# Linear attention and a top-1 mixture of experts on one core: remainders of up to 64 tokens join the chunk ahead as a fourth half tile, remainders of 65 to 192 take a tile from it, and the narrow body goes

## The chip, the cores and the metric

The kernel runs on one core of one Trainium2 chip. The metric is the device time of one execution in microseconds; the time before is 680.21 us, the median of three runs (679.69 to 680.33). Engines are named as the profile names them: PE (matmul) and PEld (its weight loads), DVE (vector), ACT (scalar), POOL (GpSimd) and SP (which issues most DMAs).

## The reference

Eight batches of eight heads with 576 positions of 64 dimensions go through a linear attention with 128 random features; the result, 4608 tokens of 512 numbers, goes through a mixture of eight experts of which each token uses the one with the largest gate logit.

```python
def phi(x):
    proj = np.einsum('bhsd,md->bhsm', x, omega)
    h = proj - np.sum(x * x, axis=-1, keepdims=True) / 2.0
    return np.exp(h - np.max(h, axis=-1, keepdims=True)) / np.sqrt(m)
q_p, k_p = phi(q * scale), phi(k * scale)
kv, z = np.einsum('bhsm,bhsd->bhmd', k_p, v), np.sum(k_p, axis=2)
num = np.einsum('bhsm,bhmd->bhsd', q_p, kv)
den = np.einsum('bhsm,bhm->bhs', q_p, z)[..., None] + 1e-06
x = (num / den), as rows of tokens (4608 x 512)
logits = x @ w_gate;  expert_idx = argmax(logits);  gate_w = softmax(logits)[expert_idx]
for e in range(8):
    ye = np.maximum(x[expert_idx == e] @ w1[e], 0.0) @ w2[e]      # 512 -> 1024 -> 512
    out[expert_idx == e] = gate_w[...] * ye
```

## The kernel before

The first part (some 245 us) is attention, one unit for each batch and head, with the gate's logits worked out beside it. Tokens are written to DRAM as rows (`token_rows`) with the softmax weight at the end. The routing ranks each token within its expert.

The second part is the experts. Tokens of an expert are cut into chunks of T3 = 384 (A3 = 3 tiles of P = 128). Chunk t's tokens are fetched by indirect DMA through a table of slots, `idx`, that `slots` makes: one-hot matrices of the tokens' slots (`T1`, line 740) are multiplied on PE with matrices that hold the tokens' numbers (`RH`, line 748). A front of T2 = 256 tokens of the expert that leads after half the batches is worked out early, in single precision, while the routing goes on. `plan` then works out flags for each chunk: its expert's number and whether it changes, whether the chunk exists, how many tokens it has. All engines load these flags into registers and branch on them.

Matmuls of the chunks run in fp32r with operands split into a high and a low part. Layer 1 (`layer1`, `wide`, `l1`) takes 96 matmuls a chunk: eight blocks of 128 features, 12 matmuls each, with n columns, where n is 384, 320 or 256 by the tokens; two blocks (a group g) share a pair of PSUM banks, `p_1[g % 2]`, which `hid` empties with ACT and DVE. A chunk of up to 192 tokens goes through the narrow body (`slim`, lines 1025 to 1029): 64 matmuls, high and low part of the tokens side by side. Layer 2 (`layer2`, line 1060) takes 24 matmuls of 512 columns a tile (`triple`), or 16 for a half tile of up to 64 tokens (`l2` with `half`); tiles of a chunk that hold no token are skipped by a branch (line 1064).

`step(t)` is layer 1 and layer 2 of a chunk on PE, then on the others the weights of chunk t+1, the gather of chunk t+3 (POOL), `begin(t+1)` and the output of chunk t (`out2`: ACT scales a whole tile; for a half tile ACT, DVE and DVE; POOL scatters the rows to the output, line 1079). `begin(t)` moves chunk t+1 through DRAM (`move`, SP), starts loads of the next expert's weights, splits new weights where the expert changes (`change`, `split`), and turns chunk t+1's rows (`xrows`, `xtrans`: a transpose on DVE, a cast on ACT, a subtraction on DVE for each tile). Where the chunk before was narrow, `xrows` waits for layer 1 of the next instead (lines 1056 to 1058).

The order on each engine is that of the program text. `Routing.constants` runs after the first unit of attention: POOL makes the iotas and masks, DVE takes token numbers from one of them (lines 474 to 478), and `clear` sets the gather buffer to zero.

Of the kernel before, what the change touches and what calls it, by code (L numbers as in the profile page):

```python
# [8 lines left out]
F32 = mybir.dt.float32  # L9
# [28 lines left out]
NCL = -(-(NT - T2) // T3)  # L38
NCH = (NT - T2 + E * (T3 - 1)) // T3
NQ = NCH + 2  # L40
NS = A3 * NCH
# [375 lines left out]
class Routing:  # L417
# [10 lines left out]
    def setup(self):  # L428
# [7 lines left out]
        self.RH = self.oh.tile([P, NLT, 2, P], BF16, name="rt_RH")  # L436
        self.EX = t("rt_EX", [P, GT, E + 1])
# [13 lines left out]
    def constants(self):  # L451
# [4 lines left out]
        nc.vector.tensor_copy(self.iob, self.iop)  # L456
        nc.gpsimd.iota(self.rev, pattern=[[-1, E]], base=E, channel_multiplier=0, allow_small_or_imprecise_dtypes=True)
# [76 lines left out]
    def group(self, bs, g, sl, lr):  # L534
# [114 lines left out]
    def head(self, nb, idx, flags):  # L649
# [5 lines left out]
        v = t("v", [P, 4 * E])  # L655
        mx, mw, io, lo = v[:, :1], v[:, 1:2], v[:, 2:4], v[:, 4:6]
        w, sel, ns = (v[:, i * E:(i + 1) * E] for i in range(1, 4))
        self.sel = sel
# [41 lines left out]
        def f6():  # L700
            nc.vector.tensor_scalar(out=ns, in0=sel, scalar1=-1.0, scalar2=1.0, op0=ALU.mult, op1=ALU.add)
            nc.vector.tensor_tensor(out=self.low, in0=self.low, in1=sel.unsqueeze(1).to_broadcast([P, E, E]), op=ALU.max)
            nc.vector.tensor_tensor(out=self.low, in0=self.low, in1=ns.unsqueeze(2).to_broadcast([P, E, E]), op=ALU.mult)
# [15 lines left out]
    def slots(self, banks, idx, fill):  # L719
# [6 lines left out]
        cnt, c2, off, m, nn = t("cnt", [P, E]), t("c2", [P, E]), t("off", [P, E]), t("m", [P, E, E]), t("nn", [P, E])  # L726
        nc.vector.scalar_tensor_tensor(out=nn, in0=self.sel, scalar=-float(T2), in1=pn[:, :E], op0=ALU.mult, op1=ALU.add)
        nc.vector.tensor_scalar(out=cnt, in0=nn, scalar1=1.0 / T3, scalar2=FLOOR3, op0=ALU.mult, op1=ALU.add)
        nc.vector.tensor_scalar(out=c2, in0=cnt, scalar1=BIG, scalar2=-BIG, op0=ALU.add, op1=ALU.add)
        cb = c2.unsqueeze(1).to_broadcast([P, E, E])  # L730
        nc.vector.tensor_tensor(out=m, in0=self.low, in1=cb, op=ALU.mult)
        nc.vector.tensor_reduce(out=off, in_=m, axis=AX.X, op=ALU.add)
        nc.vector.scalar_tensor_tensor(out=cnt, in0=off, scalar=1.5, in1=self.sel, op0=ALU.mult, op1=ALU.subtract)
        so, tt = t("so", [P, NLT, E]), t("tt", [P, NLT])
        nc.vector.tensor_tensor(out=so, in0=self.OH.rearrange("p g s e -> p (g s) e"),
                                in1=cnt.unsqueeze(1).to_broadcast([P, NLT, E]), op=ALU.mult)
        nc.vector.tensor_reduce(out=tt, in_=so, axis=AX.X, op=ALU.add)
        nc.vector.scalar_tensor_tensor(out=tt, in0=tt, scalar=2.0, in1=self.RT.rearrange("p g s -> p (g s)"),
                                       op0=ALU.mult, op1=ALU.add)
        T1 = t("T1", [P, NLT, NS], BF16)  # L740
        for c in range(0, NLT, GT):
            nc.vector.tensor_tensor(out=T1[:, c:c + GT, :], in0=tt[:, c:c + GT].unsqueeze(2).to_broadcast([P, GT, NS]),
                                    in1=self.iop[:, :NS].unsqueeze(1).to_broadcast([P, GT, NS]), op=ALU.is_equal)
        for f, eng in self.tail:
            f(eng)
        for n, pp in enumerate((pa, pb)):
            for c in range(NLT):
                nc.tensor.matmul(pp[:, :NS], self.RH[:, c, n, :], T1[:, c, :], start=c == 0, stop=c == NLT - 1)
# [3 lines left out]
        self.off, self.c2, self.nn = off, c2, nn  # L752

    def plan(self, flags):


        nc, t, inc = self.nc, self.t, self.t("inc", [1, E])
        nc.vector.tensor_tensor(out=inc, in0=self.off[:1], in1=self.c2[:1], op=ALU.add)
        ge, eq, et = t("ge", [1, NQ, E]), t("eq", [1, NQ, E]), t("et", [1, NQ])
        io = self.iop[:1, :NQ].unsqueeze(2).to_broadcast([1, NQ, E])  # L760
        nc.vector.tensor_tensor(out=ge, in0=io, in1=inc.unsqueeze(1).to_broadcast([1, NQ, E]), op=ALU.is_lt)
        nc.vector.tensor_tensor(out=eq, in0=io, in1=self.off[:1].unsqueeze(1).to_broadcast([1, NQ, E]), op=ALU.is_ge)
        nc.vector.tensor_tensor(out=eq, in0=eq, in1=ge, op=ALU.mult)
# [12 lines left out]
        nc.vector.tensor_scalar(out=nx, in0=nx, scalar1=1.0, scalar2=-1.0, op0=ALU.max, op1=ALU.mult)
        nc.vector.tensor_scalar_add(nx, nx, float(E))
        nt, en, sb = t("nt", [1, NQ]), t("en", [1, E]), t("sb", [1, NQ])
        pick = t("pick", [1, NQ, E])
        nc.vector.tensor_tensor(out=pick, in0=eq, in1=nx.unsqueeze(1).to_broadcast([1, NQ, E]), op=ALU.mult)  # L780
        nc.vector.tensor_reduce(out=nt, in_=pick, axis=AX.X, op=ALU.add)
        nc.vector.scalar_tensor_tensor(out=en, in0=self.off[:1], scalar=float(T3), in1=self.nn[:1], op0=ALU.mult, op1=ALU.add)
        nc.vector.tensor_tensor(out=pick, in0=eq, in1=en.unsqueeze(1).to_broadcast([1, NQ, E]), op=ALU.mult)
        nc.vector.tensor_reduce(out=sb, in_=pick, axis=AX.X, op=ALU.add)
        nc.vector.scalar_tensor_tensor(out=sb, in0=self.iop[:1, :NQ], scalar=-float(T3), in1=sb, op0=ALU.mult, op1=ALU.add)
        nc.vector.tensor_scalar(out=sb, in0=sb, scalar1=0.0, scalar2=float(T3), op0=ALU.max, op1=ALU.min)
        for i, a in ((0, ch), (1, nt), (2, act), (4, sb)):
            nc.vector.tensor_copy(flags[:, i, :], a)


class Experts:
# [7 lines left out]
    def __init__(self, tc, ctx, rt, xs, w1, w2, out, ident, ps):  # L799
# [8 lines left out]
        self.xg = [cp.tile([P, A3, ROW], F32, name="xg")]  # L808
# [5 lines left out]
        self.bounce = [self.nc.dram_tensor(f"chunk_rows{i}", (T3, DM), F32, kind="Internal").ap() for i in range(2)]  # L814
        gt = cp.tile([P, 2 + 2 * A3], F32, name="gt")
        self.gt = [gt[:, i:i + 1] for i in range(2 + 2 * A3)]
# [103 lines left out]

    def gather(self, t):
        for a in range(A3):
            i = A3 * t + a
            self.nc.gpsimd.indirect_dma_start(out=self.xg[t % 2][:, a, :], out_offset=None, in_=self.xs[:, :],  # L924
                                              in_offset=bass.IndirectOffsetOnAxis(ap=self.idx[:, i:i + 1], axis=0),
                                              bounds_check=NT - 1, oob_is_err=False)
# [5 lines left out]
    def gate(self, t, a):  # L932
        return self.gt[2 + t % 2 * A3 + a]

    def weigh(self, t):
        self.weights(self.xg[t % 2], [self.gate(t, a) for a in range(A3)])

    def move(self, t):

        rows = self.bounce[t % 2]
        self.nc.sync.dma_start(rows.rearrange("(a p) n -> p a n", p=P), self.xg[t % 2][:, :, :DM])
        for q in range(4):
            self.nc.sync.dma_start(self.xq[q * Q:(q + 1) * Q],
                                   rows[:, q * P:(q + 1) * P].rearrange("(a g i) n -> i a g n", a=A3, i=Q))

    def xtrans(self, t, a):

        if t < NCH:  # L950
            x = self.xg[t % 2][:, a, :DM].rearrange("p (c t) -> p c t", t=P)
# [313 lines left out]
```

## Time and profile before

| | us |
|---|---|
| median of 3 runs | 680.21 (679.69 to 680.33) |
| the profiled execution | 679.88 |
| its span, first to last instruction | 678.2 |
| PE busy | 658.5 (97%) |
| DVE, ACT, POOL busy | 376.7, 359.2, 271.4 |

The profile is one execution, in which times count from the span's first instruction. Matmuls overlap in their pipeline, so the duration of one (0.33 to 0.39 us in the expert part) is longer than the time from one's start to the next one's; the text works with starts. In a row of the timeline stand start, busy time, engine, line, operation, output and inputs with their shapes, the number of merged instructions, and in brackets the idle time before it and what ended it.

### The profile page before, as it was taken

How to read it: one execution, taken by the hardware profiler on the slowest of the kernel's cores; microseconds unless marked ns; L12 is line 12 of the kernel's file. 1: busy time of each engine (PE TensorE's matmuls, PEld its weight loads, DVE VectorE, ACT ScalarE, POOL GpSimd, SP SyncE). 2: the span in 40 equal slices, each digit the busy share in tenths (PEclk: the TensorE clock that was granted, in tenths of full speed). 3: DMA queues.
4: the chain of work that ended last, by engine and by line, in shares of the span. 5: the costliest groups of instructions: out<-in, count | busy, mean ns of one | idle time of the engine just before them, and what ended most of it. 6: DMA issues, size and time to landing. Idle time of an engine off the chain costs nothing. (4 is left out here: it accounts for less than half of the span.)

```text
span 678.2 us, 19569 instructions
## 1 busy us (share of the span) xinstructions
PE 658.5 (97%) x7011; PEld 597.8 (88%) x7011; DVE 376.7 (56%) x729; ACT 359.2 (53%) x1082; POOL 271.4 (40%) x492
## 2 busy tenths in 40 slices
PE   8999999999999999999999999999999999999994
PEld 5999999999998987989898989898989888898983
DVE  4788888888887788632513265232455257332321
ACT  4999999999998935322222244222343254222121
POOL 6545557886787775041230304122112223122122
PEclk8999999999999999999999999999999999999998
DMA  7772835728493223747633456441457274541210
GB/s 221 222 231 67 269 112 175 234 59 261 114 350 131 43 77 96 233 146 251 157 94 115 105 196 159 178 120 58 103 188 243 105 214 128 197 119 45 54 49 10
DMA packets 93105, 100.51 MB, mean 148 GB/s; under 512 B 28942, under 2 KB 73486, under 8 KB 92304
## 3 DMA queue, kind: packets, MB, share of 16 engines
q1 hardware_dynamic: 85216, 79.27, 38.7%
q0 software_dynamic: 7040, 19.04, 9.0%
q8 instruction: 89, 1.46, 0.9%
q14 instruction: 72, 0.59, 0.3%
q10 hardware_dynamic: 688, 0.16, 0.1%
HBM read 72.92 MB, written 29.77 MB: 151 GB/s over the span
## 5 line engine op out<-in xcount | busy, mean ns | idle before, releaser
L975 PE MATMUL p<-xb,w1p 128*128 128x384 f32 (+1 forms) x1056 | 183.4, 333 | 0.5 <-DVE xb L51 0.4
L975 PEld LDWEIGHTS p<-xb,w1p 128*128 128x128 f32 x1056 | 181.0, 188 | 2.3 <-issue 1.5
L1079 POOL DMA_INDIRECT out_dram<-ys,idx x38 | 38.2, 1005 | 269.4 <-DVEq L1069 79.9
L887 PE MATMUL p<-w2p,hb 128*128 128x512 f32 x552 | 127.1, 389 | 0.0
L1002 DVE SCALAR_TENSOR_TENSOR hb<-p,hb 128x768 fp32r<-128x768 f32 (+1 forms) x44 | 41.0, 932 | 154.5 <-ACTq L1110 96.3
L887 PEld LDWEIGHTS p<-w2p,hb 128*128 128x128 f32 x552 | 103.6, 188 | 21.5
L1001 ACT ACTIVATE hb<-p 128x768 fp32r<-128x768 f32 (+1 forms) x44 | 34.9, 793 | 110.0 <-PE p L975 109.7
L191 DVE TENSOR_REDUCE mx<-pp 128x8 f32<-128x1024 f32 x64 | 78.0, 1218 | 10.5 <-PE pp L185 9.8
L199 ACT ACTIVATE qp<-pp,mx 128x128 f32<-128x128 f32 x256 | 77.2, 435 | 0.0
L199 ACT ACTIVATE kp<-pp,mx 128x128 f32<-128x128 f32 x256 | 74.1, 385 | 5.0 <-DVE de L283 1.4
L185 PE MATMUL pp<-omt,th 64*128 64x128 f32 x1024 | 72.1, 281 | 0.0
L185 PEld LDWEIGHTS pp<-omt,th 64*128 64x128 f32 x1024 | 63.4, 191 | 0.0
L887 PE MATMUL p_1tr<-w2p,hb 128*128 128x512 f32 x240 | 57.0, 391 | 0.6 <-DVEq L1110 0.5
L211 POOL TENSOR_TENSOR k<-kp 128x256 f32<-128x256 f32 x64 | 46.7, 729 | 23.7 <-ACT kp L199 18.7
L887 PEld LDWEIGHTS p_1tr<-w2p,hb 128*128 128x128 f32 x240 | 44.8, 188 | 10.3 <-DVEq L1110 0.9
L176 DVE COPY th<-tr 128x512 f32<-128x512 f32 x63 | 43.3, 687 | 5.1 <-PE tr L168 3.3
L274 PE MATMUL nu<-kva,qt 128*64 128x73 f32 x1008 | 46.0, 233 | 0.0
L243 ACT COPY qt<-t 128x512 f32<-128x512 f32 x64 | 42.3, 661 | 2.0 <-PE t L168 1.5
L274 PEld LDWEIGHTS nu<-kva,qt 128*64 128x64 f32 x1008 | 36.7, 136 | 4.2
L225 PE MATMUL kf<-kp,v 128*64 128x128 f32 x512 | 39.4, 275 | 0.0
L924 POOL DMA_INDIRECT xg<-token_rows,idx x24 | 26.4, 1100 | 30.2 <-DVEq L1110 17.3
L57 ACT CAST xb<-xgm 128x512 fp32r<-128x512 f32 x21 | 13.0, 621 | 45.6 <-DVE xgm L952 44.7
(387 smaller groups left out, 1063.4 us busy)
## 6 DMA issues: line engine op xcount, KB each, us to landing
w1s<-in_moe_w_dram SPq DMA_DIRECT2D x5, 2048.0 KB, 8.6
w2s<-in_moe_w_dram SPq DMA_DIRECT2D x5, 2048.0 KB, 11.0
xq<-chunk_rows SPq DMA_DIRECT2D x52, 192.0 KB, 4.3
v<-in_v_dram SPq DMA_DIRECT2D x32, 256.0 KB, 5.7
token_rows<-x SPq DMA_DIRECT2D x8, 1024.0 KB, 8.4
k<-in_k_dram SPq DMA_DIRECT2D x31, 256.0 KB, 5.2
q<-in_q_dram SPq DMA_DIRECT2D x31, 256.0 KB, 5.5
chunk_rows<-xgm SPq DMA_DIRECT2D x7, 768.0 KB, 4.6
```

The costliest lines, as they stand in the source:

```text
L176: self.nc.vector.tensor_copy(t.rearrange("p n (a t) -> p a n t", a=2), s[("tr", h)])
L185: nc.tensor.matmul(o[:, a, n, :], t[r, n, :], self.om[r], start=True, stop=True)
L191: self.nc.vector.tensor_reduce(out=mx, in_=s[("pp", h)], axis=AX.X, op=ALU.max, negate=True)
L199: self.nc.scalar.activation(o[:, j, :], p[:, a, 2 * n + i, :], AF.Exp, bias=mx[:, a, 2 * n + i:2 * n + i + 1])
L211: nc.gpsimd.tensor_tensor(out=k2, in0=kp[:, :2, :], in1=kp[:, 2:, :], op=ALU.add)
L225: nc.tensor.matmul(pkv[c * D:(c + 1) * D, :M], vv, kk, start=n < 2, stop=n > 2)
L243: self.nc.scalar.copy(qt.rearrange("p n (a t) -> p a n t", a=2), s[("t2", h)])
L274: nc.tensor.matmul(o[r, j, :], qt[:, j, r], kva[:, h if h >= 0 else 2 * j + a, :], start=True, stop=True)
L887: self.nc.tensor.matmul(p, x, w[:, c, :], start=c == 0 and x is h and w is self.w2h, stop=c == self.NF - 1 and x is l)
L975: self.nc.tensor.matmul(o, w[:, c, k], x[:, c, :], start=i == 0, stop=i == len(ops) - 1)
L1002: self.nc.vector.scalar_tensor_tensor(out=l, in0=p, scalar=0.0, in1=h.bitcast(F32), op0=ALU.max, op1=ALU.subtract)
L1079: self.nc.gpsimd.indirect_dma_start(out=self.out[:, :], in_=y, in_offset=None, bounds_check=NT - 1, out_offset=bass.IndirectOffsetOnAxis(a ...
```

## The change

- The chunks: an expert's remainder of up to 64 tokens behind its last full chunk joins that chunk as a half tile (T4 = 448 columns, `idx` gets a slot for each chunk's half tile, `p_2` a fourth bank, `gather`, `weigh`, `move`, `xrows` and `out2` a fourth part). A remainder of 65 to 192 is made larger: the chunk ahead gives one tile of 128 to it.
- `slim`, `l1_both` and `hid_both` go; layer 1 has bodies of 384, 448, 320 and 256 columns.
- The routing (`slots`): more small operations find the chunks' counts; the one-hot matrix is transposed, in bf16, and compared with a table `sn` that POOL makes in `constants`.
- `plan` is cut into three pieces; two of them run between the groups of chunk 0's layer 1. The load of the next expert's w1 is issued after that layer.
- `xrows(t + 1)` stands in `begin` without a condition.
- `hb` and `hq` move to a pool of their own, `h0` shares the memory of `xq`.

```diff
+T4 = T3 + HT
-NCL = -(-(NT - T2) // T3)
+NCL = -(-(NT - T2 - (E - 1) * HT) // T3)
-NS = A3 * NCH
+NM = A3 * NCH
+NS = NM + NCH
...
     def constants(self):
         nc.vector.tensor_copy(self.iob, self.iop)
+        nc.gpsimd.tensor_copy(self.sn[:, :NM], self.iop[:, :NM].unsqueeze(2).to_broadcast([P, NM, NLT]))
+        nc.gpsimd.tensor_scalar(out=self.sn[:, NM:], in0=self.iop[:, 1:NCH + 1].unsqueeze(2).to_broadcast([P, NCH, NLT]),
+                                scalar1=float(A3), scalar2=64.0, op0=ALU.mult, op1=ALU.add)
...
-            self.tail = [(f, nc.vector if i % 2 == 0 or i == 17 else nc.scalar if i < 8 else nc.gpsimd)
+            self.tail = [(f, nc.scalar if i % 2 and i < 12 else nc.vector if i < 16 and i % 2 == 0 else nc.gpsimd)
...
     def slots(self, banks, idx, fill):
+        for i, k in enumerate((1.0, 64.0)):
+            nc.scalar.activation(so[:, i, :, E:E + 1], rank.unsqueeze(2), AF.Copy, scale=k)
+        V.scalar_tensor_tensor(out=cnt, in0=self.sel, scalar=float(HT - T2), in1=pn[:, :E], op0=ALU.mult, op1=ALU.add)
...
+        V.scalar_tensor_tensor(out=X[:, 1], in0=b, scalar=8192.0, in1=c1, op0=ALU.mult, op1=ALU.add)
+        for i in range(2):
+            V.tensor_tensor(out=so[:, i, :, :E], in0=oh, in1=X[:, i].unsqueeze(1).to_broadcast([P, NLT, E]), op=ALU.mult)
+        for i in range(2):
+            V.tensor_reduce(out=v2[:, i], in_=so[:, i, :, :E + 1], axis=AX.X, op=ALU.add)
...
-        T1 = t("T1", [P, NLT, NS], BF16)
-        for c in range(0, NLT, GT):
-            nc.vector.tensor_tensor(out=T1[:, c:c + GT, :], in0=tt[:, c:c + GT].unsqueeze(2).to_broadcast([P, GT, NS]),
-                                    in1=self.iop[:, :NS].unsqueeze(1).to_broadcast([P, GT, NS]), op=ALU.is_equal)
+        for c in range(0, NLT, 2 * GT):
+            V.tensor_tensor(out=T1[:, :, c:c + 2 * GT], in0=tt[:, c:c + 2 * GT].unsqueeze(1).to_broadcast([P, NS, 2 * GT]),
+                            in1=self.sn[:, :, c:c + 2 * GT], op=ALU.is_equal)
...
     def gather(self, t):
-        for a in range(A3):
+        for a in range(A3 + (t > 0)):
...
     def xrows(self, t):
-        for a in range(A3):
+        for a in range(A3 + 1):
             self.xtrans(t, a)
...
     def layer1(self, t):
-            self.either(r > T2, lambda: self.either(r > T3 - HT, wide(T3), wide(T3 - HT)),
-                        lambda: self.either(r > T2 - HT, wide(T2), lambda: self.slim(t, g)))
+            self.either(r > T3 - HT, lambda: self.either(r < T3 + 1, wide(T3), wide(T4)),
+                        lambda: self.either(r > T2, wide(T3 - HT), wide(T2)))
             if g == 1 and t == 1:
                 self.xrows(t + 1)
-            elif g == 1:
-                with self.tc.If(self.before < T2 - HT + 1):
-                    self.xrows(t + 1)
...
     def layer2(self, t):
+        if t:
+            with self.tc.If(self.r4 > T3):
+                self.l2(A3, True)
         for a in range(A3 - 1, 0, -1):
             with self.tc.If(self.r4 > a * P):
                 one(a)
...
     def begin(self, t):
         if 1 < t < NCH - 1:
-            with self.tc.If(self.r2 > T2 - HT):
-                self.xrows(t + 1)
+            self.xrows(t + 1)
...
     def step(self, t, following):
         if t == 0:
-            self.first(T3)
+            self.first(T3, self.pieces)
+            self.next(0, 1)
...
-        for a in range(A3 - 1, -1, -1):
+        for a in range(A3 - (t == 0), -1, -1):
             self.out2(t, a, r, r2)
```

## Rows read from the trace of the kernel before

**Rows 1.** The page: engines' busy time; wide layer 1's group.
```profile
PE 658.5 (97%) x7011; PEld 597.8 (88%) x7011; DVE 376.7 (56%) x729; ACT 359.2 (53%) x1082; POOL 271.4 (40%) x492
...
L975 PE MATMUL p<-xb,w1p 128*128 128x384 f32 (+1 forms) x1056 | 183.4, 333 | 0.5 <-DVE xb L51 0.4
```
**Rows 2.** Timeline of PE, chunk 6 into chunk 7.
```profile
468.86 16.83 PE L975 MATMUL p<-xb,w1p 128*128 128x384 f32 x96
485.52 5.64 PE L887 MATMUL p_1tr<-w2p,hb 128*128 128x512 f32 x24
...
501.88 16.83 PE L975 MATMUL p<-xb,w1p 128*128 128x384 f32 x96
```
**Rows 3.** The same, chunk 3 (303 tokens) into chunk 4, where the expert changes.
```profile
373.80 14.24 PE L975 MATMUL p<-xb,w1p 128*128 128x320 f32 x96
387.88 3.81 PE L1036 MATMUL p_1tr<-w2p,hq 128*128 128x512 f32 x16
...
402.41 17.22 PE L975 MATMUL p<-xb,w1p 128*128 128x384 f32 x96
```
**Rows 4.** The same, the last chunk: end of layer 1, and layer 2.
```profile
664.37 0.36 PE L982 MATMUL p<-xb,w1p 128*128 128x384 f32 x1
665.61 3.94 PE L1036 MATMUL p<-w2p,hq 128*128 128x512 f32 x16 [0.87 <-PEq L1064]
```
**Rows 5.** Timeline of DVE behind the last matmul.
```profile
670.35 0.68 DVE L1092 TENSOR_TENSOR yt<-p,yt 64x512 f32<-64x512 f32 x1 [3.30 <-ACT yt L1091]
671.12 0.48 DVE L1093 TENSOR_SCALAR ys<-yt,gt 64x512 f32<-64x512 f32 x1
```
**Rows 6.** Timeline of PE, chunk 8 (narrow): layer 1 into layer 2.
```profile
544.33 0.36 PE L982 MATMUL p<-xb,w1p 128*128 128x384 f32 x1
545.33 3.94 PE L1036 MATMUL p<-w2p,hq 128*128 128x512 f32 x16 [0.64 <-PEq L1064]
```
**Rows 7.** Line 1064 on PE's queue, in 544:546 and 663:667 (ns min/median/max, first, last).
```profile
L1064 PEldq EVENT_SEMAPHORE  x1: 51/51/51, 544.7 to 544.7; - x1
L1064 PEldq COMPARE_BRANCH  x1: 70/70/70, 544.9 to 544.9; - x1
...
L1064 PEldq COMPARE_BRANCH  x2: 208/1090/1973, 662.3 to 664.9; - x2
L1064 PEldq EVENT_SEMAPHORE  x2: 51/51/51, 664.8 to 665.2; - x2
```
**Rows 8.** Timeline of POOL at the start: iotas, memset of the gather buffer.
```profile
5.68 0.25 POOL L455 IOTA rt_iop<- 128x128 f32 x1
...
7.95 0.33 POOL L471 IOTA rt_id<- 64x4 int32 x2
8.33 1.40 POOL L809 MEMSET xg<- 128x1560 f32 x1
```
**Rows 9.** Timeline of DVE there: the first operation on rt_id.
```profile
9.34 0.49 DVE L474 TENSOR_SCALAR rt_part<-rt_id 128x36 int32<-128x36 int32 x1
```
**Rows 10.** Timeline of PE there.
```profile
11.22 0.34 PE L168 MATMUL tr<-ident,k 64*128 64x64 f32 x4 [1.96 <-DVE th L176]
```
**Rows 11.** Groups of POOL's instructions by form: busy, mean ns | idle before.
```profile
L631 POOL TENSOR_SCALAR rt_RH<-rt_iob,rt_RM,rt_ihi 128x128 bf16<-128x128 bf16 x23 | 18.4, 798 | 0.1
```
**Rows 12.** Timeline of DVE in the routing, from the count to the one-hot.
```profile
248.30 0.23 DVE L588 TENSOR_TENSOR m<-rr,rt_OH 128x72 f32<-128x72 f32 x1 [0.73 <-PE rr L515]
...
250.25 0.46 DVE L735 TENSOR_TENSOR f_so<-rt_OH,f_cnt 128x288 f32<-128x288 bf16 x1
...
251.46 2.60 DVE L742 TENSOR_TENSOR f_T<-f_tt,rt_iop 128x513 bf16<-128x513 f32 x4
```
**Rows 13.** Timeline of PE there: the slots' matmuls.
```profile
255.22 2.25 PE L748 MATMUL p<-f_T,rt_RH 128*128 128x57 bf16 x72
```
**Rows 14.** Timeline of DVE: two tiles of xrows before chunk 7.
```profile
492.67 1.08 DVE L952 STREAM_TRANSPOSE xg<-xq 128x512 f32<-128x512 f32 x1
...
495.05 1.07 DVE L952 STREAM_TRANSPOSE xg<-xq 128x512 f32<-128x512 f32 x1
```

More of the change, by code (lines that the diff above doesn't have):

```diff
@@ new lines, in changes, with following @@
+        def changes():
+            T(out=ge, in0=eq, in1=self.iop[:1, :E].unsqueeze(1).to_broadcast(wide), op=ALU.mult)
+            V.memset(ch[:, :1], 0.0)
+            add(et, ge)
+            T(out=ch[:, 1:], in0=et[:, 1:], in1=et[:, :NQ - 1], op=ALU.not_equal)
+            T(out=flags[:, 0, 1:], in0=ch[:, 1:], in1=act[:, 1:], op=ALU.mult)
+            V.tensor_copy(flags[:, 0, :1], ch[:, :1])
+        def following():
+            V.tensor_single_scalar(nx, c2, 0.5, op=ALU.is_gt)
+            T(out=e8, in0=nx, in1=self.rev[:1], op=ALU.mult)
+            T(out=mm, in0=self.upp[:1], in1=e8.unsqueeze(1).to_broadcast([1, E, E]), op=ALU.mult)
+            V.reduce_max(out=nx, in_=mm, axis=AX.X)
+            V.tensor_scalar(out=nx, in0=nx, scalar1=1.0, scalar2=-1.0, op0=ALU.max, op1=ALU.mult)
+            V.tensor_scalar_add(nx, nx, float(E))
+            T(out=pick, in0=eq, in1=be(nx), op=ALU.mult)
+            add(nt, pick)
+            V.tensor_copy(flags[:, 1, :], nt)
@@ L791 @@
+        return [found, changes, following]
 class Experts:
@@ L1002, in high_low, with first @@
         self.nc.vector.scalar_tensor_tensor(out=l, in0=p, scalar=0.0, in1=h.bitcast(F32), op0=ALU.max, op1=ALU.subtract)
-    def hid_both(self, g, n, k):
-        nc, f = self.nc, slice(2 * g, 2 * g + 2)
-        p, y = self.p_1[g % 2][:, :, :2 * n].rearrange("p f (s t) -> p f s t", t=n), self.hs[g % 2]
-        nc.scalar.copy(y, p[:, :, 1])
-        nc.vector.tensor_tensor(out=y, in0=p[:, :, 0], in1=y, op=ALU.add)
-        if k:
-            self.whole(f, k, y[:, :, :k])
-        self.half(f, y[:, :, k:k + HT])
-    def first(self, n):
+    def first(self, n, pieces):
         for g in range(self.NF // 2):
@@ L1018, in first @@
             self.wide(0, g, n)
+            if pieces:
+                pieces.pop(0)()
     def wide(self, t, g, n):
@@ L1096, in both @@
             if t == 0:
-                self.store(p, g, self.idx[:, i:i + 1])
+                self.store(p, g, i)
                 return
             y = self.y()
-            self.either(r2 > a * P + HT, lambda: nc.scalar.activation(y, p, AF.Copy, scale=g), lambda: half(y))
-            self.scatter(y, self.idx[:, i:i + 1])
+            if a < A3:
+                self.either(r2 > a * P + HT, lambda: nc.scalar.activation(y, p, AF.Copy, scale=g), lambda: half(y))
+            else:
+                half(y)
+            self.scatter(y[:self.span(a)], i)
         if a:
@@ L1211, in run @@
         self.move(1)
-        rt.plan(self.flags)
-        self.next(0, 1)
+        found, *self.pieces = rt.plan(self.flags)
+        found()
         for t in range(NCL - 1):
```

180 lines of the change are left out of this document (90 added, 90 removed).

## The prediction

> **What bounds the kernel now.** I read the page first, then the timeline of PE, then what stands before PE's few gaps. PE is busy 97% of the span, and 1056 matmuls of a wide layer 1 at 96 a chunk make 11 wide chunks [rows 1]. The rest of layer 1 is two narrow chunks. This agrees with the tokens, which I counted with the reference on its drawn inputs: 1711, 1152, 576 and 1169 for four experts. 256 of the first run ahead as chunk 0's front, so 1455 = 3x384+303, 1152 = 3x384, 576 = 384+192, 1169 = 3x384+17: 13 chunks, numbered 0 to 12 here.
>
> In the timeline of PE chunk 6 starts at 468.86 and chunk 7 at 501.88 with no gap: 16.66 us for layer 1, 16.36 for layer 2 [rows 2]. So a wide chunk is PE alone, 0.1735 us a matmul of 384 columns and 0.2272 for one of 512. The chunk of 303 runs with 320 columns: 14.08/96 = 0.1467 a matmul, 28.61 us in all [rows 3]. The two sizes give 0.00042 us a column; 256 columns should cost 0.120, 448 should cost 0.200. What PE does is what the end moves by, except where PE stands: at the first copies of attention, at the routing, at an expert's change, behind a skipped branch.
>
> **The chunks, what is gained.** The new rule gives 4, 3, 2 and 3 chunks: 576 becomes 256+320, and the last expert 384, 384, 448 (17 tokens in the half tile). Nothing changes before chunk 7. There, from 501.88 to the last matmul's end, 665.61+3.94 = 669.55 [rows 2, 4], stand 167.67 us. After:
> - 256: 96x0.120 + 48x0.2272 = 22.41.
> - 320: 28.61, as chunk 3.
> - 384 after a change of expert behind a 320: its layer 1 lasts 17.22 where 16.83 is usual [rows 2, 3], so 33.41. Then 384: 33.02.
> - 448: 96x0.2004 + 88x0.2272 = 19.24+19.99, and 0.16 for the last matmul's own end: 39.39.
>
> The sum is 156.8, a gain of 10.8. Layer 2 has as many matmuls as before, 344. Behind the last matmul the half tile needed ACT, DVE, DVE; now tile 0 is whole and ACT alone scales it. The two DVE operations, 0.68 and 0.48 with a handover of 0.09, go [rows 5]: 1.2. Gain 12.0.
>
> **Skips on PE, the largest cost.** layer2 now begins with a branch on r4 > T3 that only the 448 chunk takes; chunks 1 to 10 skip it. The trace has such skips on PE only in the narrow chunks. In the first the last layer-1 matmul starts at 544.33 and the next matmul at 545.33, idle 0.64 before it, put down to PE's queue at line 1064 [rows 6]. The rows of that line show why: a semaphore event at 544.7, just as the last matmul ends (544.33+0.36), then a branch at 544.9; with two skips there are two such events and 0.87 idle [rows 4, 7]. I read it so: a skipped body must post its semaphore, and the post waits until PE has run dry. All of PE's matmuls are queued behind it, and everything waits for PE. Start to start is 1.00 against a usual 0.17: 0.83 for one skip, 1.24-0.17 = 1.07 for two. About 0.14 of it is the taken jump into the half body (208 ns against 70 in the branch rows), which a 384 chunk doesn't make. So 0.69 for nine chunks, 0.14 more for the 320 of the new chunk 8, and 0.93 for the 256, which skips two: 6.2+0.15+0.9 = 7.3. Bounds: 5.2 if only the recorded idle counts (10x0.50+0.2), 8.5 at 0.83 each. A loss of nothing is a rival, below.
>
> **The constants, at the start.** Two operations enter POOL's queue between the iotas of rt_iop (5.68) and rt_id (until 8.28): a copy of 57x36 = 2052 elements and a multiply-add of 684. DVE's constants read rt_id, and behind them in DVE's order stands a copy of attention (line 176) for which PE already waits 1.96 us at 11.22 [rows 8 to 10]. Nothing hides this: the longer POOL takes, the later that copy. Price of the copy: the memset of 1560 at 1.40 gives 0.84 ns an element with its start, 1.9 us. The multiply-add: by the memset 0.8; by POOL's tensor_scalar of 128 elements at 0.80 us [rows 11], about 4.7 ns an element behind its start, 3.4. I take the middle, 2.0; X = 3.9. The first DVE constant on rt_id took 0.49 for 36 elements and ended at 9.83, as POOL's memset did (8.33+1.40) [rows 8, 9]. So DVE either waits for the iota alone (X-1.35 = 2.5) or for the grown memset too (X+0.46 = 4.4). I take 3.5; bounds 1.0 and 5.7.
> [...]
>
> **The routing.** From the count to the first one-hot operation DVE now has 13 small operations for 6, two products and two sums for one each, three closing ones for one. Before, the products began 1.95 us after the first operation at 248.30, with 16 small operations interleaved (some 0.13 each), and the one-hot at 251.46 [rows 12]. Seven more at 0.14 are 1.0, the second product and sum about 0.75, two more at the end 0.25: the one-hot starts 2.0 later. It has 2736 elements for 2052. The row gives 0.65 us for 513, so two of 1368 would be 3.1 at its rate; DVE's scaling of 512 elements in 0.48 [rows 5] is the cheapest rate of a row, giving 2.1. Between them I take 2.6, as long as before. PE reached line 748 at 255.22 without a wait [rows 13]; its later matmuls need the tail's rows, which DVE makes behind the one-hot, one fewer for PE's first half than before, so of the 2.0 I take 1.7 for PE. Bounds 0.5 and 2.6. Gather and turning follow idx and shift as a whole.
> [...]
>
> **A change of expert.** xrows turns a fourth, half tile. A tile takes 2.38 (492.67 to 495.05) [rows 14], the half some 1.3. Beside a wide layer 2 this is hidden; before chunk 4, and before the new chunk 9, DVE and ACT are late already (the 0.39 above). There 1.3 and a little ACT branch work come on top, while PE comes 0.8 later through its skip: 0.75 each, 1.5 together; bounds 0 and 2.8.
>
> **Edits costed at nothing.** The fourth gather and weight copy, and one more issue on SP: POOL is busy 40% [rows 1] and the gathers run two chunks ahead; if that cover went, each gather costs POOL about 1 us. The plan's pieces move behind layer 1's groups of chunk 0, where DVE has time. w1's load for the next expert is issued later on SP, behind move(1); its first reader is the split before chunk 4, at 402.41. h0 shares xq, so move(1)'s second step waits for layer 2 of the front, whose matmuls end before chunk 0 begins. Dropping the conditional xrows inside layer1 frees xq and xg earlier. The larger memset of xg[1] and the fourth gather delay only chunk 1's rows, a chunk ahead.
>
> **Sum.** -12.0+7.3+3.5+1.7+1.5 = +2.0 us. The profiled execution took 679.88 (span 678.2 and 1.7 around it), 0.33 below the median 680.21; on the median the change comes to 682.2.
>
> **Rivals.**
> 1. The new skip is free behind 384 columns, because PE's sequencer runs far enough ahead. For it: chunk 3 jumps into the half body with no gap [rows 3]. Against it: the event falls on the end of the last matmul both times. Then 682.2-7.3 = 675. It decides at 0.5 us a skip: below that the kernel is faster. Chance 0.17.
> 2. [...] Chance 0.20.
> 3. The stalls are dear: POOL's multiply-add at tensor_scalar's price and DVE held until the memset's end, 5.7 in place of 3.5; the routing at 2.6 for 1.7, the changes of expert at 2.8 for 1.5: 686.6. For it: the one tensor_scalar of size on POOL has that price. Chance 0.13.
> 4. The counts differ on the chip and 13 chunks stay: the gain is gone, some 692. Against it: the shapes of the trace fit the counts. Chance 0.03.
>
> **How the numbers follow.** The forecast has 0.47. About 0.2% (1.36 us) is what a measurement of this kernel can tell from no change: under 678.85 or over 681.57. Around 682.2 I give the forecast 0.29 slower, 0.15 within, 0.03 faster; rival 1 gives 0.15 faster and 0.02 within; rival 2 0.09 and 0.11; rivals 3 and 4 are slower. Faster 0.27, within 0.28, slower 0.45. The range 676 to 687 leaves out about half of rival 1, rival 4 and the edge of rival 3.
>
> **What would show it.** Chunks 1 to 10 of the new trace with a gap of about 0.5 between layer 1 and layer 2, put down to PE's queue, and ten events on that line: right; seamless chunks: rival 1. PE's gap near 11.22 grown from 2 to 5.5 us with DVE waiting for POOL: the start. A gap at line 748 of 1 to 2 us: the routing. 12 chunks, the last with 448 columns, and 157 us plus skips from the 256 chunk to PE's end: the gain. The prediction is wrong if skips cost under 0.5, or if a wait appears that no row of before has, such as DVE's xrows holding the 256 chunk.

## The result, and the profile after

The changed kernel takes 689.85 us (median of 4 runs, 689.28 to 690.62) against 679.95 beside it: a ratio of 1.0146, 95% interval 1.0129 to 1.0164. It is 9.9 us slower. The forecast was 682.2 with a range of 676 to 687: the sign is right, the size is not, and the time lies outside the range. The profiled execution took 690.15 us, with a span of 688.3 where the kernel before had 678.2; the 10.1 us between the spans can be taken apart at five points that both traces have.

| stretch | before | after | difference | forecast |
|---|---|---|---|---|
| start, to the count's matmul | 248.19 | 251.52 | +3.33 | +3.5 |
| routing, from there to layer 1 of chunk 0 | 20.10 | 30.25 | **+10.15** | **+1.7** |
| chunk 0 | 38.85 | 38.85 | 0 | 0 |
| chunks 1 to 6 | 194.74 | 198.37 | +3.63 | +4.9 |
| chunk 7 to the last matmul's end | 167.67 | 161.40 | -6.27 | -6.9 |
| behind it | 8.65 | 7.91 | -0.74 | -1.2 |

Five of the six terms came out within 1.3 us, though the first of them moves by more than a microsecond between profiles of the same start (see "The start" below). One, the routing, is 8.5 us off, which is about the whole error. The timeline of PE of the kernel after shows where (start us, duration us, engine, line, operation; lines are those of the new kernel: L771 is the old L748, L900 the old L859), with three rows of the kernel before behind it:

```profile
251.52 0.18 PE L733 MATMUL p<-rt_CU,rt_ones 128*128 128x8 bf16 x1
251.56 7.15 PE L900 MATMUL p<-x,w1s 128*128 128x256 f32 x32
258.55 10.56 PE L771 MATMUL p<-rt_T,rt_RH 128*128 128x76 bf16 x72
268.93 5.10 PE L900 MATMUL p<-x,w1s 128*128 128x256 f32 x12
273.87 4.46 PE L918 MATMUL p<-w2s,xq 128*128 128x512 f32 x10
...
248.19 0.18 PE L724 MATMUL p<-rt_CU,rt_ones 128*128 128x8 bf16 x1
257.31 2.84 PE L859 MATMUL p<-x,w1s 128*128 128x256 f32 x12
259.98 4.45 PE L877 MATMUL p<-w2s,h 128*128 128x512 f32 x10
```

From the count to the first slot matmul PE takes 7.03 us, exactly as before, and starts line 771 with no wait. But the 72 slot matmuls take 10.56 us where [rows 13] had 2.25, and the 12 layer-1 products behind them take 5.10 where the kernel before had 2.84. From start to start that is 10.38 for 2.09 and 4.94 for 2.67, +8.29 and +2.27; what stands between them and chunk 0 took 0.41 less (7.90 for 8.31), which makes the 10.15. VectorE did its part faster than the cheapest rate I had from a row (2.1), 1.65 us for the one-hot that took 2.60 in [rows 12], and its last row of the tail was there at 259.81:

```profile
256.36 1.65 DVE L765 TENSOR_TENSOR rt_T<-f_tt,rt_sn 128x1368 bf16<-128x1368 bf16 x2
```

Stretches of 2 us there (PE busy, weight loads, DVE, ACT and POOL with counts, then the granted clock, DMA share, GB/s):

```profile
260.00:262.00 2.00, 2.00 (x16) 1.65 (x15) 0.00 (x0) 0.00 (x0) 0.00 (x0) 1.00 0.00 0
...
264.00:266.00 2.00, 2.00 (x16) 1.79 (x15) 0.00 (x0) 0.00 (x0) 0.00 (x0) 0.50 0.03 8
...
274.00:276.00 2.00, 2.00 (x6) 0.82 (x5) 0.92 (x4) 1.94 (x6) 2.00 (x2) 1.00 0.63 173
```

And stretches of 3 us of line 771 alone (PE busy, weight loads, granted clock, DMA share, GB/s):

```profile
259.00:262.00 3.00, 3.00 (x23) 2.47 (x22) 1.00 0.00 0
...
264.00:267.00 3.00, 3.00 (x23) 2.69 (x22) 0.50 0.02 5
```

From 260 to 268 all other engines are idle, hardly anything is moved (DMA share 0.00 to 0.03), PE counts as busy throughout, and a stretch of 3 us touches 23 slot matmuls at a granted clock of 1.00 and 23 at 0.50. The rate of these matmuls did not change when the granted clock was halved. The halved clock does cost something afterwards: the 12 layer-1 products, at a granted clock of 0.50 to 272 and a mean of 0.60 from there to 274, take 0.41 us each from start to start, where the kernel before took 0.22 at 1.00. I read this as a "busy" PE waiting for its operand, which the profile doesn't call idle; the experiments test it.

The other stretches came out near the forecast. The start, on POOL and then on DVE:

```profile
5.99 1.90 POOL L461 CAST rt_sn<-rt_iop 128x2052 bf16<-128x2052 f32 x1
7.86 0.78 POOL L462 TENSOR_SCALAR rt_sn<-rt_iop 128x684 bf16<-128x684 f32 x1
11.03 1.83 POOL L850 MEMSET xg<- 128x2080 f32 x1
...
11.00 1.89 DVE L481 TENSOR_SCALAR rt_part<-rt_id 128x36 int32<-128x36 int32 x1 [1.50 <-POOL rt_id L478]
```

And the chunks: the skip in a chunk of 384 between layer 1 and layer 2, the 256, and the last one with 448 columns, after which a single ACT operation stands where [rows 5] had two of DVE:

```profile
372.00 5.71 PE L928 MATMUL p_1tr<-w2p,hb 128*128 128x512 f32 x24 [0.44 <-PEq L1081]
...
518.99 11.67 PE L1022 MATMUL p<-xb,w1p 128*128 128x256 f32 x96
531.75 11.18 PE L928 MATMUL p<-w2p,hb 128*128 128x512 f32 x48 [1.08 <-ACTq L1133]
...
640.59 19.61 PE L1022 MATMUL p<-xb,w1p 128*128 128x448 f32 x96
660.05 4.00 PE L1057 MATMUL p_1t<-w2p,hq 128*128 128x512 f32 x16
...
680.55 0.69 ACT L1121 ACTIVATE ys<-p,gt 128x512 f32<-128x512 f32 x1 [4.75 <-PE p L928]
```

### The profile page after: what moved, and what is told of

It is laid out like the page before. It is cut to its first block, busy times and chain, and to the rows that moved or that the text cites. A ratio compares the mean times of both kernels' runs of the same rounds, so it can differ in the third digit from the quotient of the medians.

```text
span 688.3 us, 19314 instructions
## 1 busy us (share of the span) xinstructions
PE 662.6 (96%) x6979; PEld 597.7 (87%) x6979; DVE 382.0 (55%) x755; ACT 359.3 (52%) x1089; POOL 283.3 (41%) x514
## 5 line engine op out<-in xcount | busy, mean ns | idle before, releaser
L1022 PE MATMUL p<-xb,w1p 128*128 128x384 f32 (+3 forms) x1152 | 195.1, 329 | 0.0
L1022 PEld LDWEIGHTS p<-xb,w1p 128*128 128x128 f32 x1152 | 191.5, 188 | 3.1 <-issue 0.8
L928 PE MATMUL p<-w2p,hb 128*128 128x512 f32 x576 | 132.6, 389 | 1.1 <-ACTq L1133 1.1
L1038 DVE SCALAR_TENSOR_TENSOR hb<-p,hb 128x768 fp32r<-128x768 f32 (+1 forms) x48 | 42.8, 891 | 157.4 <-ACTq L1133 80.9
L928 PEld LDWEIGHTS p<-w2p,hb 128*128 128x128 f32 x576 | 108.0, 188 | 23.7 <-ACTq L1133 1.3
L1037 ACT ACTIVATE hb<-p 128x768 fp32r<-128x768 f32 (+1 forms) x48 | 36.4, 759 | 109.3 <-PE p L1022 81.3
L928 PE MATMUL p_1tr<-w2p,hb 128*128 128x512 f32 x216 | 51.5, 393 | 3.2 <-PEq L1081 3.1
L928 PEld LDWEIGHTS p_1tr<-w2p,hb 128*128 128x128 f32 x216 | 39.9, 188 | 13.8 <-issue 4.5
L971 POOL DMA_INDIRECT xg<-token_rows,idx x31 | 32.4, 1045 | 22.4 <-DVE idx L774 14.1
L59 ACT CAST xb<-xgm 128x512 fp32r<-128x512 f32 (+1 forms) x24 | 13.6, 567 | 48.2 <-DVE xgm L999 43.8
```

What stands on the lines that cost most here:

```text
L928: self.nc.tensor.matmul(p, x, w[:, c, :], start=c == 0 and x is h and w is self.w2h, stop=c == self.NF - 1 and x is l)
L1022: self.nc.tensor.matmul(o, w[:, c, k], x[:, c, :], start=i == 0, stop=i == len(ops) - 1)
L1038: self.nc.vector.scalar_tensor_tensor(out=l, in0=p, scalar=0.0, in1=h.bitcast(F32), op0=ALU.max, op1=ALU.subtract)
```

## The experiments

**Theory.** The new one-hot T1 is stored [slots, token columns]. VectorE writes it in runs of 18 adjoining elements, but a slot matmul takes one token column of it, `T1[:, :, c]`, so that its 76 columns lie 36 elements of bf16, 72 bytes, apart. Before, `T1[:, c, :]` gave 57 columns side by side. **Rivals:** the 19 more columns, the later rows of the tail, or the longer chain of small operations.

### The layout turned back for TensorE alone

```
-        self.T1 = self.oh.tile([P, NS, NLT], BF16, name="rt_T1")
+        self.T1 = self.oh.tile([P, NLT, NS], BF16, name="rt_T1")
...
-            V.tensor_tensor(out=T1[:, :, c:c + 2 * GT], in0=...
+            V.tensor_tensor(out=T1[:, c:c + 2 * GT, :].rearrange("p c s -> p s c"), in0=...
...
-                nc.tensor.matmul(pp[:, :NS], self.RH[:, c, n, :], T1[:, :, c], ...
+                nc.tensor.matmul(pp[:, :NS], self.RH[:, c, n, :], T1[:, c, :], ...
```

> The kernel after, with one change: the one-hot T1 is stored slot by slot within each token column, so that the 76 columns which one slot matmul reads lie side by side, as the kernel before had them; VectorE writes them through a turned view. Theory (the stride is the price): in the kernel after each slot matmul reads its 76 columns 72 bytes apart, and that made the 72 matmuls take 10.56 us instead of 2.25 and let the granted clock fall behind them. Side by side they take 76/57 of 2.25 us, 3.0 us, the clock stays at 1.00, the 12 layer-1 products behind them are back from 5.10 to 2.84 us, and the time falls by 9 to 10.5 us, to 679.5 to 681. VectorE's comparison may go back from 1.65 to 2.6 us for its scattered writes. Rival (the 19 more columns, or the later half-tile rows of the right operand, hold TensorE): the matmuls still span over 8 us and the time stays at 688 to 691.

Measured: 690.43 us, 1.0153 (1.0132 to 1.0175): no gain at all. By its total the rival would stand. The timelines of DVE and PE, and a stretch of 2 us at a granted clock of 0.50, say otherwise:

```profile
256.99 11.87 DVE L765 TENSOR_TENSOR rt_T<-f_tt,rt_sn 128x1368 bf16<-128x1368 bf16 x2
...
263.07 1.32 PE L771 MATMUL p<-rt_T,rt_RH 128*128 128x76 bf16 x18 [3.75 <-DVE rt_T L765]
268.91 3.87 PE L771 MATMUL p<-rt_T,rt_RH 128*128 128x76 bf16 x54 [4.52 <-DVE rt_RH L638]
...
270.00:272.00 2.00, 2.00 (x29) 1.76 (x29) 0.29 (x2) 0.00 (x0) 0.00 (x0) 0.50 0.00 0
```

TensorE now needs 3.71 us for 54 matmuls (to 272.62, where the next begin), 0.069 each on average, nearly all of it at a granted clock of 0.50, where the kernel after needed 0.144 (the clock fell here while TensorE stood waiting: a mean of 0.56 in 262 to 264, with the first slot matmul at 263.07). But VectorE, which now writes 152 bytes from element to element, needs 11.87 us for 1.65, and TensorE waits for it twice. The price moved from the reader to the writer. Taking 2.6 us as the dear end for VectorE here was the same oversight as in the prediction, one engine on.

### The kernel before with the turned layout

```
-        T1 = t("T1", [P, NLT, NS], BF16)
+        T1 = t("T1", [P, NS, NLT], BF16)
...
-            nc.vector.tensor_tensor(out=T1[:, c:c + GT, :], in0=...
+            nc.vector.tensor_tensor(out=T1[:, :, c:c + GT].rearrange("p s c -> p c s"), in0=...
...
-                nc.tensor.matmul(pp[:, :NS], self.RH[:, c, n, :], T1[:, c, :], ...
+                nc.tensor.matmul(pp[:, :NS], self.RH[:, c, n, :], T1[:, :, c], ...
```

> The kernel before, with the one-hot T1 alone turned as in the kernel after: the 57 columns of a slot matmul lie 72 bytes apart. All else is the kernel before. Theory (the stride): the kernel after took some 0.14 us for a matmul of 76 columns, 1.9 ns a column, whether the clock was granted at 1.00 or at 0.50; 72 matmuls of 57 columns then span 7.8 us instead of 2.25, +5.5 us, and if the clock falls behind them here too, up to 2.3 us more: 685 to 688. Rival (number of columns or the new routing's operations): no change, 679.5 to 681.

Measured: 689.95 us, 1.0148 (1.0115 to 1.0182). With the old counts, the old chunks and 57 columns this one change of layout costs the kernel before as much as the whole change did; the number of columns and the new operations are out as causes. It is 2 us more than the upper end expected. Here both sides stride: VectorE's comparison writes 72 bytes apart, and TensorE reads so, and in the profile TensorE waits 1.13 and 1.15 us for VectorE between its slot matmuls. From the count (249.84) to layer 1 of chunk 0 (280.29) pass 30.45 us, 10.35 more than in the kernel before and close to the kernel after's 30.25.

```profile
253.12 9.15 DVE L742 TENSOR_TENSOR f_T<-f_tt,rt_iop 128x513 bf16<-128x513 f32 x4
...
256.87 2.08 PE L748 MATMUL p<-f_T,rt_RH 128*128 128x57 bf16 x18
```

9.15 us for the 2.60 of [rows 12], and 0.116 us a matmul (18 in 2.08) for the 0.031 of [rows 13].

### How far apart is too far

The 36 token columns in three thirds, stored so that VectorE's writes always adjoin while TensorE's 76 columns lie 24, 8 and 4 bytes apart:

```
+        w = [flat[:, i * q * NS:(i + 1) * q * NS].rearrange("p (g s c) -> p g s c", s=NS, c=k)
+             for i, k in enumerate((12, 4, 2))]
...
+                nc.tensor.matmul(pp[:, :NS], self.RH[:, c, n, :], w[0][:, 0, :, c], ...
...
+                nc.tensor.matmul(pp[:, :NS], self.RH[:, q + c, n, :], w[1][:, c // 4, :, c % 4], ...
...
+                nc.tensor.matmul(pp[:, :NS], self.RH[:, 2 * q + c, n, :], w[2][:, c // 2, :, c % 2], ...
```

> The kernel after with T1 stored in three ways, 12 of the 36 token columns each: the 76 slots that a slot matmul reads lie 24, 8 and 4 bytes apart. VectorE writes each third with its own one operation, whose writes run on without a gap in all three. TensorE's 24 matmuls of each third, and VectorE's operation on each, have a line of their own. Theory A (a price of any column that does not lie beside the last): all three thirds cost TensorE about the 0.115 to 0.145 us a matmul of 72 bytes, 24 matmuls some 3 us each. Theory B (the price grows with the bytes between columns, until each column is a fetch of its own): 4 bytes near the 0.035 to 0.07 us of adjoining columns, 8 bytes between, 24 bytes near 0.12. VectorE: as its writes adjoin, each third takes 0.55 us (a third of 1.65); a run of only 2 or 4 elements may cost it the fast rate, 0.9 to 1.2 us (a third of 2.6 us times 76/57). One look at the parts; total between 682 and 690.

The timeline of PE (24, 8, 4 bytes, then the next product), and VectorE's three operations for them:

```profile
258.94 1.79 PE L777 MATMUL p<-rt_T,rt_RH 128*128 128x76 bf16 x12
260.56 1.02 PE L779 MATMUL p<-rt_T,rt_RH 128*128 128x76 bf16 x12
261.40 0.60 PE L781 MATMUL p<-rt_T,rt_RH 128*128 128x76 bf16 x12
...
264.74 2.83 PE L911 MATMUL p<-x,w1s 128*128 128x256 f32 x12
...
256.77 0.63 DVE L768 TENSOR_TENSOR rt_T<-f_tt,rt_sn 128x912 bf16<-128x912 bf16 x1
257.32 0.63 DVE L769 TENSOR_TENSOR rt_T<-f_tt,rt_sn 128x912 bf16<-128x912 bf16 x1
257.86 0.99 DVE L771 TENSOR_TENSOR rt_T<-f_tt,rt_sn 128x912 bf16<-128x912 bf16 x1
```

From start to start a matmul takes 0.135 us at 24 bytes, 0.070 at 8 and 0.037 at 4 (the last start to start with the second pass, 261.84). Theory B: the price grows with the bytes between columns, 4 bytes cost no more than side by side (0.037 us for 76 columns, 0.029 for the 57 of the kernel before, 0.0005 a column both times), and 72 bytes at 0.144 are hardly worse than 24. The clock stayed at 1.00 in every stretch of 2 us from 254 to 274, and the products behind took 2.83. The whole took 683.87 in a single run. VectorE keeps its quick rate with runs of 12 and of 4 elements (0.55 us from start to start for 912, a third of the 1.65 for 2736) and loses a good part of it with runs of 2 (0.91).

### Both sides side by side

T1 as the kernel before had it, for writer and reader, with the token column's number spread along the slots; the 2736 slot numbers shrink to one row of 76:

```
+        self.T1 = self.oh.tile([P, NLT, NS], BF16, name="rt_T1")
+        self.sn = self.oh.tile([P, NS], BF16, name="rt_sn")
...
+            V.tensor_tensor(out=T1[:, c:c + 2 * GT, :], in0=tt[:, c:c + 2 * GT].unsqueeze(2).to_broadcast([P, 2 * GT, NS]),
+                            in1=self.sn.unsqueeze(1).to_broadcast([P, 2 * GT, NS]), op=ALU.is_equal)
```

> The kernel after with the one-hot's layout of the kernel before: the 76 slots of a token column side by side for TensorE and for VectorE's writes, the column's number spread over the slots in VectorE's operand; the slot numbers are one row of 76 in place of 2736, so that GpSimd's 2.68 us at the start go too. Theory (the turned layout cost 10.6 us, on TensorE by its reads and on VectorE if it writes across): VectorE's comparison takes 2.6 x 76/57 = 3.5 us, the 72 matmuls 3 us once their rows are there, some 2 us of waiting for them, clock at 1.00 or a short fall: 7 to 9 us less in the routing. The start gains 2.7 to 3.3 us, as VectorE's first token operation comes as early as before and nothing of GpSimd's stands behind the clearing. 678 to 681. Rival (the routing's longer chain of small operations costs the time whatever the layout): the routing gains under 4 us, 683 to 687.

Measured: 680.01 us, 1.0008 (0.9986 to 1.003): without its layout and without GpSimd's 2736 slot numbers the change is worth nothing either way. The timelines of DVE and PE, then stretches of half a microsecond of line 771 alone:

```profile
255.89 3.08 DVE L765 TENSOR_TENSOR rt_T<-f_tt,rt_sn 128x1368 bf16<-128x1368 bf16 x2
258.89 1.88 DVE L638 TENSOR_SCALAR rt_RH<-rt_iob,rt_RM,rt_ihi 128x128 bf16<-128x128 bf16 x8
...
258.07 0.80 PE L771 MATMUL p<-rt_T,rt_RH 128*128 128x76 bf16 x18
259.02 3.31 PE L771 MATMUL p<-rt_T,rt_RH 128*128 128x76 bf16 x54 [0.15 <-DVE rt_T L765]
262.17 2.83 PE L900 MATMUL p<-x,w1s 128*128 128x256 f32 x12
...
259.50:260.00 0.50, 0.47 (x4) 0.25 (x3) 1.00 0.00 0
260.00:260.50 0.50, 0.47 (x3) 0.21 (x3) 1.00 0.00 0
261.00:261.50 0.50, 0.50 (x19) 0.50 (x16) 1.00 0.00 0
```

From the count (251.04) to layer 1 of chunk 0 (273.09) pass 22.05 us, 1.95 more than before. That is what I had put down for the routing, 1.7, and by the mechanism that I had: from start to start the 72 slot matmuls take 4.10 us for 2.09. VectorE's one-hot, now 3.08 us, holds TensorE for 0.15, and the tail's rows behind it for longer: while VectorE makes them, to 260.77, TensorE touches three or four slot matmuls in half a microsecond, and 19 once they are there. In this profile the count itself still came late (251.04 for 248.19), though GpSimd's work was gone; in three other runs with the one row it came at 248.73 to 249.43.

### GpSimd's slot numbers behind the clearing

```
-        nc.gpsimd.tensor_copy(self.sn[:, :NM], ...)        (in constants, behind the first iota)
+    def slot_numbers(self):                                (called behind pre.clear())
+        nc.gpsimd.tensor_copy(self.sn[:, :NM], ...)
```

> The kernel after, with GpSimd's two operations that make the slot numbers put behind all other constants and behind the clearing of the gathered rows. Theory (GpSimd's order at the start): VectorE's first operation on the token numbers is back at about 9.3 us, the copy behind it at 10.5 instead of 13.55, and the time falls by 2.7 to 3.3 us, to 686.5 to 687.2. Rival (GpSimd's work holds VectorE wherever it is put): the two operations, 2.68 us, now run from about 10.2 to 12.9 beside VectorE's copies out of PSUM and stretch them; of the gain under 1 us is left, 689 to 690.

Measured: 689.77 us (687.41 to 691.8), 1.0156 (1.0125 to 1.0187): no gain can be told from these runs. In the profile, which is of the fastest of them, VectorE's copy comes at 12.98 for 13.55, 0.6 us earlier. POOL, then DVE:

```profile
8.32 1.83 POOL L854 MEMSET xg<- 128x2080 f32 x1
10.09 1.90 POOL L487 CAST rt_sn<-rt_iop 128x2052 bf16<-128x2052 f32 x1
11.98 0.76 POOL L488 TENSOR_SCALAR rt_sn<-rt_iop 128x684 bf16<-128x684 f32 x1
...
9.22 1.02 DVE L479 TENSOR_SCALAR rt_part<-rt_id 128x36 int32<-128x36 int32 x1
10.28 1.75 DVE L480 CAST rt_ihi<-rt_part 128x36 f32<-128x36 int32 x1
12.07 0.71 DVE L481 TENSOR_SCALAR rt_ihi<-rt_ihi 128x36 f32<-128x36 f32 x1
```

Three of VectorE's operations on 36 elements, 0.18 us where GpSimd rests, end at 10.24, 12.03 and 12.78: as GpSimd's three end at 10.15, 11.99 and 12.74. None of them needs GpSimd's results by then. The rival holds: at their new place, too, GpSimd's operations hold up VectorE's beside them. With the one row of 76 slot numbers the transposes that wait for this copy began at 12.16 us against 14.29 in the kernel after and 11.22 in [rows 10], so the work has to go, not move.

### The half tile's branch in tile 2's

```
-        if t:
-            with self.tc.If(self.r4 > T3):
-                self.l2(A3, True)
         for a in range(A3 - 1, 0, -1):
             with self.tc.If(self.r4 > a * P):
-                one(a)
+                if t and a == A3 - 1:
+                    self.either(self.r4 > T3, four, lambda: one(a))     (four: half tile, then tile 2)
+                else:
+                    one(a)
```

> The kernel after, with the half tile's branch on TensorE moved into tile 2's: behind the branch of tile 2 stands one choice of two bodies, half tile and tile 2, or tile 2 alone, so that no empty branch of its own is passed. Theory (an empty branch drains TensorE): the 0.67 us ahead of the third tile goes in the chunks of 384, some of the two in the chunks of 320 and 256, and chunk 4 gets back the 0.39 us that it waited before; in all 6 to 7 us less, 683 to 684. Rival (the pause is the price of any choice, or the program grows and its fetch takes it back): under 1.5 us is gained, 688.3 to 690.5.

Measured: 686.87 us, 1.0104 (1.0082 to 1.0125): 3.0 less than the kernel after, between the two expectations. The cost of a skip is shown: the plain chunks of 384 are back from 33.70 to 33.03, and layer 2 follows layer 1 without a gap. What was not expected is where half of it went. Timeline of PE, chunk 2 and then chunk 4:

```profile
354.04 16.83 PE L1022 MATMUL p<-xb,w1p 128*128 128x384 f32 x96
370.71 5.64 PE L928 MATMUL p_1tr<-w2p,hb 128*128 128x512 f32 x24
...
415.84 8.51 PE L1022 MATMUL p<-xb,w1p 128*128 128x384 f32 x48
425.97 8.59 PE L1022 MATMUL p<-xb,w1p 128*128 128x384 f32 x48 [1.62 <-DVE hb L1038]
```

Where the expert changes, TensorE now waits 1.62 us in chunk 4 and 1.59 in chunk 9 in the middle of layer 1, for VectorE's low part of the first group. In the kernel after the empty branches had held TensorE back so that this was not seen: from the start of chunk 1 to the end of chunk 4 pass 130.97 us there and 130.86 here, so what chunks 2 and 3 gained, chunk 4 gave back.

### Without the half tile's rows

```
-        for a in range(A3 + 1):
+        for a in range(A3 + (t > 10)):
             self.xtrans(t, a)
```

> The kernel after with the merged branch, and VectorE's and ScalarE's turning and splitting of the half tile's rows left out for the chunks 1 to 10, where it is empty with these inputs (a branch that is decided when the kernel is built; other inputs would need the rows). With the merged branch alone TensorE waited 1.6 us for VectorE's low parts inside layer 1 of the chunks 4 and 9, those that change the expert, and the chunks gave back some 3.5 of the 6.5 us of the empty branches. Theory (the half tile's rows are VectorE's excess there): those waits go back to under 0.4 us each, and the time falls 2 to 3.5 us below the merged branch alone, 683.3 to 685. Rival (the waits come of the splitting of the new weights alone, or of the choice of bodies): no change, 686.4 to 687.3.

Measured: 684.54 us, 1.0071 (1.0046 to 1.0096), some 2.2 below the merged branch by the ratios, each against its own runs of before, and 1.6 by the medians; the intervals overlap. In the profile chunk 4's wait fell to 0.91, chunk 9's went, chunk 1 took 33.33 us for 34.14, and from chunk 1 to the last matmul's end passed 354.2 us for 357.3. So turning and splitting the half tile's rows costs something once the skips don't hide it, but how much isn't shown: chunk 1 is clear, while the waits in chunks 4 and 9 differ as much between two profiles of one kernel (1.18 and 1.48, then 0.81 and 0.94, in the two runs of the next section without a branch around these rows). Why chunk 4 keeps more than the 0.39 of before stays open.

### Put together

> The run with the old layout and one row of slot numbers, and the half tile's branch merged into tile 2's on TensorE besides. If the parts add up: the run without the merged branch less the 3.0 us that the merged branch gave alone, 675 to 678, below the kernel before. Rival: TensorE waits for VectorE in the chunks anyway, and what the start and the routing gave is taken back in the chunks: within 1 us of the run without the merged branch.

Measured: 676.88 us, 0.9962 (0.995 to 0.9975). The two parts add up: 3.1 below the run with the old layout alone, and below the kernel before.

With the half tile's rows under a branch at run time besides, and the kernel without it again beside it:

```
+            with self.tc.If(self.reg(4, t, T4, (ET.Activation, ET.DVE)) > T3):
+                self.xtrans(t, A3)
```

> The kernel of the old layout, one row of slot numbers and the merged branch, and VectorE's and ScalarE's turning and splitting of the half tile's rows put under a branch on the next chunk's count (a decision at run time, so it holds for any inputs). With the half tile's rows left out when the kernel was built, the waits for VectorE in layer 1 fell from 1.62 and 1.59 to 0.91 and 0, chunk 1 became 0.8 us shorter and chunk 9 1.7 us, some 3.2 us in all. Theory (the rows are the excess, and two engines that pass an empty branch lose less than the rows took, 0.3 to 0.7 us a chunk beside TensorE): 1 to 3 us below the same kernel without this branch, 674 to 676. Rival (an empty branch drains VectorE and ScalarE as it does TensorE, in every chunk, and they are what the chunks with a new expert wait for): no gain or up to 1.5 us lost.

> The kernel of the old layout, one row of slot numbers and the merged branch once more, on the chip of the run with the branch around the half tile's rows, to stand beside it: 0.4% below the kernel before as it was, 676 to 677.5 where that stands at 679 to 680.

Measured: 673.75 us, 0.9931 (0.9916 to 0.9945), and 675.42, 0.9953 (0.9937 to 0.9969). The branch gains 1.7 us in the medians, though the intervals overlap; in the profiles it is chunk 1 that shows it, 33.09 us for 34.12, and chunk 4 still waits, 0.96 for 0.81. This version is 0.7% faster than the kernel before: the chunks' gain was there, and the side costs had eaten it (the one-hot's layout, GpSimd's slot numbers, the skips, the half tile's rows).

## Why the prediction was wrong, step by step

- **The routing: the step that failed.** I worked out VectorE's part of it with care and wrote that "PE reached line 748 at 255.22 without a wait", and then took its 72 matmuls to be as long as before. The diff turned `T1[:, c, :]` into `T1[:, :, c]`, and no row of before had a strided operand on TensorE. The sum has no term for the stride, and none for 19 more columns. That asked for bounds from both sides, not for the old number. Measured: the 72 matmuls took 8.29 us more, of which the columns are some 0.6 (an estimate: 72 times 0.037 of the 4-byte third less 0.029 of before) and the stride the rest; the 12 products behind them, at the granted clock of 0.50 to 0.60, took 2.27 more in this profile, and 1.15 to 1.65 more in the three others of the same routing. The forecast gap of 1 to 2 us at this line did not come, since the slow reads were slower than the tail's rows; the 1.7 itself was sound, as the 1.95 with the old layout shows. With 1.95 in place of the 10.15 the six terms add up to 1.9, for the forecast's 2.0; that it comes so near is partly luck, as the next points show.
- **The one-hot on VectorE.** I took 2.6 us; it was 1.65. It bought nothing here, since TensorE's reads were slower (10.38 us for the 72 matmuls); with the old layout VectorE's 3.08 us and the tail behind it are what TensorE waits for, and the whole is still 8.2 us shorter.
- **The start: right in size, by two errors that cancel.** +3.33 for 3.5; at the transposes themselves, 3.07 (14.29 for 11.22). POOL's copy took the 1.90 forecast. Its multiply-add took 0.78, the memset's price, where I had 2.0 between 0.8 and 3.4. And VectorE was held to the end of the grown memset (11.00+1.89 = 12.89, the memset 12.86), where I had taken the middle between held and not held. One pair of profiles says little of this stretch: with the start of the kernel before the count came at 248.19 and 249.84 (the run with the turned layout), with that of the kernel after at 251.52 to 253.49 in five profiles, with the one row of slot numbers at 248.73 to 251.04 in four. Their means, 249.0, 252.2 and 249.5, bear out some 3 us for GpSimd's work.
- **The skips: right.** 0.67 in a plain chunk of 384 for 0.69. In the 256 and the 320 behind it the recorded waits are longer (1.08, put down to ACT's queue, and 1.22, to PE's), so chunk 7 took 23.78 for 23.34 and chunk 8 30.11 for 29.44; in the other runs that kept the empty branch chunk 8 took 29.45 to 29.73.
- **A change of expert: not seen.** I had 0.75 on top of the skip in chunks 4 and 9. In the kernel after the skip and the wait cover one another: chunk 4 grew by only 0.28 in all, which is most of what chunks 1 to 6 stayed below the forecast. With the merged branch chunk 4 takes 34.92, 1.5 more than before.
- **The gain: right.** Twelve chunks, the last one of 448. From chunk 7 to PE's end 161.4 us, forecast 156.8+3.9 = 160.7. The tail gave 0.74 for 1.2.
- **The rivals.** None of them was this one. Rival 3 had the right sign and no price above 2.6 for the routing. Rival 2 had the multiply-add at the memset's price, which it took (0.78), and for the routing 0.8, a term that no run shows: the routing took 10.15 more, and 1.95 with the old layout on both sides. It falls with that and with VectorE's wait for the memset's end (12.86). Rival 1 falls with the 0.67, rival 4 with the counts.

## What to carry to other kernels

When a diff turns the layout of a tile, price every engine that touches it, writer and readers, by the distance between the elements that one instruction takes in its innermost loop: here VectorE's comparison took 11.87 us for 1.65, and a matmul of 76 columns 0.144 for 0.037. A TensorE that counts as 100% busy can be held up by the layout of its operand, as here: look at the matmuls in a stretch, not at its busy share, and compare them at both levels of the granted clock (23 in 3 us at 1.00 and at 0.50). And after taking away a stall look at what it was hiding: here the empty branches covered VectorE's lateness, and taking them away alone paid 3.0 us of the 6 to 7 expected.

## What was not expected of the hardware

- A matmul of 76 bf16 columns took 0.037 us from start to start with the columns 4 bytes apart, 0.070 at 8, 0.135 at 24 and 0.144 at 72; at 72 bytes a stretch of 3 us touched 23 of them at a granted clock of 1.00 and as many at 0.50.
- During the slow matmuls of the kernel after the granted clock fell to 0.50 though PE counted as busy throughout. In the run with thirds and in two runs with the old layout on both sides (680.01 and 676.88 us) every stretch of 2 us from 254 to 274 had 1.00.
- VectorE's comparison into bf16 took 0.60 us per thousand elements when it wrote them in runs of 18 side by side and 4.3 when it wrote the same ones 152 bytes apart.
- A branch with an empty body on TensorE cost 0.67 us in a chunk of 384, while a choice of two bodies that both have work showed no gap (chunk 2, layer 2 at 370.71 behind layer 1's end at 370.87).
